# Attention followed by a rational feed-forward: x of two batches kept as one float32 plane, split into rounded part and remainder only in the feed-forward

## The chip, the core and the metric

The kernel runs on one core of a Trainium2 chip. The metric is the device time of one execution in microseconds (us), as the median of several runs.

## What is computed

Four batches of 448 tokens, 12 heads of 64, all float32. The scores of all heads are mixed by a 12x12 matrix before the softmax and again after it; the feed-forward has 768 -> 2048 -> 768 with a quotient of two polynomials as its activation.

```python
scores = scale * np.matmul(q, k.transpose(0, 1, 3, 2))
scores = np.einsum('bhij,hg->bgij', scores, w_pre)
attn = np.exp(scores - np.max(scores, axis=-1, keepdims=True))
attn = attn / (np.sum(attn, axis=-1, keepdims=True) + 1e-09)
attn = np.einsum('bhij,hg->bgij', attn, w_post)
x = np.matmul(attn, v)            # -> [1792, 768] after moving the heads
h = x @ w_in
P = a[0] + a[1]*h + a[2]*h**2 + a[3]*h**3
Q = 1.0 + abs(b[0])*abs(h) + abs(b[1])*h**2
out = (P / (Q + 1e-6)) @ w_out
```

## The kernel before

**Two parts.** Attention goes over 16 tiles T of query rows (`T // 4` is the batch b; a batch has three tiles of 120 rows and a short one, the first in batch 0, the last in the others). A tile has 6 groups of two blocks (a short one 5), 92 groups in all, each with one `put_pre` (mix before the softmax, L599), the softmax, and one `put_post` (mix after it, L674). `put_qk` (L498) makes the scores of a coming tile, `d<-st` DMAs of SP (L520) shuffle them into the tile `d`, and `put_av` (L739) multiplies with v, three times a tile, the first time two groups after the tile's own groups. The feed-forward then goes over 64 units u, u = 0 to 63: four chunks c of hidden columns, in each chunk four turns (one batch each, in the order of the list `orders`), in each turn four units of 128 hidden columns.

**x and its two planes.** The feed-forward multiplies in float32r, with an operand in two parts: a rounded plane hi and a remainder plane lo = x - hi. A unit's first product `m1` (18 matmuls, L918) uses both planes of x of one batch. In `put_av` ACT (ScalarE) rounds the result out of PSUM into hi (`hi`, L236) and DVE (VectorE) subtracts it to make lo (`lo`, L757). Both planes of a batch, 2688 KB, are stored by SP to `x_scr[b]`, in eight DMAs (L762). `xs` is one buffer, so a batch can write its x only when the stores of the batch before are done.

**Loads in the feed-forward.** `put_load_x` (L899) loads both planes of a turn's batch in one DMA of 2688 KB. There are two homes, the tile `xs` and the tile `d` of attention; `held` and `homes` say which load serves which turn. Turn 0 uses load 1 (into `d`), turn 1 the last batch of attention, still in `xs`, turn 2 load 2 (into `d`, free after turn 0's last m1), turn 3 load 3 (into `xs`, free after turn 1's last m1). So units 0 to 3 are turn 0, units 8 to 11 are turn 2, units 12 to 15 turn 3.

**A unit's chain.** m1 -> on ACT m, sq, ua (L931, L934, L937) and the denominator (L941) -> DVE -> Ln and Exp on ACT (L954, L958) -> DVE -> g, rounded (L236 or L238) and remainder (L978) -> six second products `m2` of three matmuls each (L1008) into the banks ps_t, ps_u, ps_a, which hold a turn's output. At a turn's end ACT or DVE copy the output to tiles `o`; in chunk 0 SP stores them to `o_scr`, in chunks 1 and 2 GpSimd (POOL) adds them there with an accumulating DMA (L1059), and the last chunk adds them on DVE.

**Order.** Nothing is scheduled at run time. Each operation is recorded with a duration, dependencies and a wished time `at`; `Plan.run` lists them per engine, lets operations that may run on ACT or DVE go where they start first, and the program is written in that order. Each engine, and SP's and POOL's queue of DMAs, then runs its list strictly in order.

```python
orders = [(0, 3, 1, 2), (2, 1, 0, 3), (3, 0, 1, 2), (2, 1, 0, 3)]
held = [1, 0, 2, 3, 3, 2, 4, 5, 5, 4, 6, 7, 7, 6, 8, 9]
```

Of the kernel before, what the change touches and what calls it, by code (L numbers as in the profile page):

```python
# [18 lines left out]
B, H, S, D = 4, 12, 448, 64  # L19
# [9 lines left out]
NT = 4 * B  # L29
# [3 lines left out]
KD = DM // 128  # L33
# [21 lines left out]
class Plan:  # L55
# [163 lines left out]
def dma(nbytes):  # L219
    return nbytes / 300e3  # L220
# [21 lines left out]
def mixed_attention_then_rational_ffn(ctx: ExitStack, tc, q, k, v, w, wmix, mask, a, b2, out):  # L242
# [481 lines left out]
    def put_av(T, pr, at):  # L724

        b, n, r, c0 = T // 4, rows[T], real[T], row0[T]
        if pr == 0:
            sums[T] = {}, [R["ps_" + holds[T]].take() for _ in range(2)]
        box, slots = sums[T]
# [14 lines left out]
        def part(hv):  # L744
            return box[hv][:, 0:3 * n].rearrange("p (r w) -> p r w", r=3)[:, :, 0:r]

        def hi(hv):
            def fn(eng):
                if hv == 0 and T % 4 == 0:
                    Xs[b] = sb["xs"].tile([128, 2, 2, 3, S], F32R, tag="xs", name="xs")  # L750
                move(nc, eng, Xs[b][:, hv, 0, :, c0:c0 + r], part(hv))
            return fn

        def lo(hv):
            def fn():
                x = Xs[b][:, hv, :, :, c0:c0 + r]
                nc.vector.tensor_sub(x[:, 1], part(hv), x[:, 0].bitcast(F32))  # L757
            return fn

        def store(hv, hl, cols):  # L760
# [9 lines left out]
            return  # L770
        for hv in range(2):
            deps, after = [o], []
            if hv == 0 and T % 4 == 0:
                deps.append(R["xs"].take())
            else:
                after.append(xs_op[b][0])
            h_ = add(copies(3 * n, False, on=ON["x_hi"]), 0, hi(hv), deps, at=at, after=after)
            l_ = add("dve", dve(3 * n), lo(hv), [h_], at=at)
            xs_op.setdefault(b, []).append(h_)
            x_done.setdefault((b, hv), []).append(l_)  # L780
            R["ps_" + holds[T]].uses[slots[hv].k].append(l_)
            if T % 4 > 1:
                last = T % 4 == 3
                cols, done = (slice(c0, S), x_done[b, hv][3:]) if last else (slice(0, c0 + r), x_done[b, hv][:])
                for hl in range(2):
                    when = at + (3.0 if last else 5.0) + (1.6 if last else 4.0) * (2 * hl + hv)
                    s_ = bulk(0.45, store(hv, hl, cols), done, at=when, nbytes=128 * 3 * max(cols.stop - cols.start, 240) * 4, late=1.0, since=when - 1.0)
                    x_st.setdefault(b, []).append(s_)
                    R["xs"].uses[b + 1].append(s_)

    xs_op, x_done = {}, {}
    x_st = {}

    LEAD = {1: 15.0, 2: 9.0, 3: 15.0}
    put_warm(8, -20.0)
# [66 lines left out]
    x_use = {0: R["xs"].uses[B]}  # L862
    x_ld[0] = x_done[B - 1, 0] + x_done[B - 1, 1]
    o_use, o_st = {}, {}
    m1_op = {}
# [25 lines left out]
    def put_load_x(n, at):  # L891
        b, name = homes[n]

        def fn():
# [265 lines left out]
```

## Time and profile before

| what | value |
|---|---|
| median of 3 runs (lowest to highest) | 826.3 us (825.48 to 827.0) |
| the profiled execution's own time | 822.94 us |
| its span, first to last instruction | 821.2 us |
| granted TensorE clock, mean of the span | 0.998 |
| busy: PE, DVE, ACT, POOL | 799.4, 692.3, 502.0, 223.7 us |
| moved by DMA | 155.46 MB |

The profiled execution is 1.7 us longer than its span, and 3.4 us under the median of the runs. Shares of busy time are means over two unlike parts: attention fills the first 340 us, the feed-forward the rest. A matmul's duration as listed overlaps that of its neighbours, so the distance between two starts tells more than the sum.

### The profile page before, as it was taken

Reading aid. Unit: us, or ns where it says so; the run is one execution under the profiler, and the core shown is the slowest. Engines: PE = TensorE matmul, PEld = TensorE weight load, DVE = VectorE, ACT = ScalarE, POOL = GpSimd, SP = SyncE. Lnnn points to the kernel's source line nnn. Section 1 sums busy time; section 2 is a strip of 40 time slices with the busy share of each in tenths; the row PEclk is TensorE's granted clock in tenths of the full one; section 3 lists DMA queues with packets and bytes.
Section 4 is the critical chain, followed back from the end, with each engine's and each line's share of the span. In section 5 each row is a group of like instructions: output and inputs, shape, how many; then the busy total and the mean of one; then the engine's idle time right before and its main releaser. Section 6 shows DMA issues by size and latency. Waiting matters only on the chain.

```text
span 821.2 us, 23269 instructions
## 1 busy us (share of the span) xinstructions
PE 799.4 (97%) x9368; PEld 598.1 (73%) x9368; DVE 692.3 (84%) x1252; ACT 502.0 (61%) x1099; POOL 223.7 (27%) x394
## 2 busy tenths in 40 slices
PE   7899999999999999999999999999999999999998
PEld 2245555554454454689999999999999999999997
DVE  6777788888887888788999998999989998777775
ACT  2557666656665666666777776677657676545632
POOL 2334444434343445611211212222212222100000
PEclk9999999999999999999999999999999999999999
DMA  6777887668877865974733275656467534466314
GB/s 219 254 215 235 259 280 236 209 199 281 266 212 210 269 192 189 352 243 192 257 126 100 75 255 126 188 124 125 84 215 212 152 81 67 94 221 224 128 52 157
DMA packets 72332, 155.46 MB, mean 189 GB/s; under 512 B 12608, under 2 KB 53152, under 8 KB 71072
## 3 DMA queue, kind: packets, MB, share of 16 engines
q1 hardware_dynamic: 68468, 142.47, 52.6%
q0 software_dynamic: 3456, 11.01, 8.2%
q8 instruction: 74, 1.21, 0.6%
q10 hardware_dynamic: 300, 0.48, 0.2%
q14 instruction: 34, 0.28, 0.1%
HBM read 77.49 MB, written 37.75 MB: 140 GB/s over the span
## 4 chain that ended last, share of the span: by engine, by line
PE 87%; DVE 5%; DMA 3%; ACT 2%; issue 1%; POOL 1%; SPq 0%; ACTq 0%; POOLq 0%; DVEq 0%
PE ps_s L918 29%; PE ps_u L1008 10%; PE ps_t L1008 9%; PE ps_a L1008 9%; PE ps_s L498 8%; PE ps_a L674 8%; PE ps_u L599 4%; PE ps_t L599 4%; PE ps_u L739 3%; PE ps_t L739 2%; ACT e L614 2%; DVE nm L605 2%; DMA d<-st 1%; DVE aa L690 1%; DMA kk<-in_k 1%
## 5 line engine op out<-in xcount | busy, mean ns | idle before, releaser
L690 DVE STREAM_TRANSPOSE aa<-ps_a 128x448 f32<-128x448 f32 (+1 forms) x184 | 107.7, 618 | 11.7 <-PE ps_a L674 11.2
L918 PE MATMUL ps_s<-d,w 128*128 128x448 f32 x504 | 107.3, 366 | 0.0
L918 PE MATMUL ps_s<-xs,w 128*128 128x448 f32 x504 | 107.1, 366 | 0.0
L447 POOL TENSOR_TENSOR w<-cm,w 128x384 fp32r<-128x384 f32 x48 | 56.0, 1167 | 171.9 <-ACT w L236 165.0
L918 PEld LDWEIGHTS ps_s<-d,w 128*128 128x128 f32 x504 | 94.3, 188 | 8.8 <-issue 0.7
L918 PEld LDWEIGHTS ps_s<-xs,w 128*128 128x128 f32 x504 | 94.6, 188 | 7.9
L634 POOL TENSOR_SCALAR krs<-kpost,rr 128x64 f32<-128x64 f32 x180 | 80.8, 462 | 69.2 <-DVE rr L625 48.0
L674 PEld LDWEIGHTS ps_a<-e,krs 64*32 64x32 f32 x2880 | 44.9, 106 | 74.7 <-issue 26.6
L674 PE MATMUL ps_a<-e,krs 64*32 64x224 f32 x2880 | 93.2, 355 | 1.5 <-DVE aa L690 0.8
L236 ACT COPY st<-ps_s 120x448 f32<-120x448 f32 (+1 forms) x115 | 57.6, 533 | 57.8 <-PE ps_s L498 30.5
L931 ACT ACTIVATE m<-ps_s,a_sb 128x448 f32<-128x448 f32 x64 | 46.3, 723 | 76.1 <-PE ps_s L918 72.7
L498 PE MATMUL ps_s<-kk,q 64*64 64x448 f32 x696 | 90.2, 548 | 0.3 <-DVE st L238 0.3
L1008 PE MATMUL ps_u<-g,w 128*128 128x448 f32 x336 | 84.1, 366 | 0.0
L1008 PE MATMUL ps_a<-g,w 128*128 128x448 f32 x336 | 84.1, 366 | 0.0
L1008 PE MATMUL ps_t<-g,w 128*128 128x448 f32 x336 | 83.9, 366 | 0.0
L614 ACT ACTIVATE e<-ps_t,nm 128x448 f32<-128x448 f32 x92 | 57.7, 634 | 31.1 <-DVE nm L605 28.0
L614 ACT ACTIVATE e<-ps_u,nm 128x448 f32<-128x448 f32 x88 | 55.2, 633 | 28.9 <-DVE nm L605 24.6
L1008 PEld LDWEIGHTS ps_t<-g,w 128*128 128x128 f32 x336 | 63.1, 188 | 5.3
L1008 PEld LDWEIGHTS ps_a<-g,w 128*128 128x128 f32 x336 | 63.1, 188 | 5.2
L1008 PEld LDWEIGHTS ps_u<-g,w 128*128 128x128 f32 x336 | 63.1, 188 | 5.2
L961 DVE TENSOR_TENSOR sq<-sq,ua 128x448 f32<-128x448 f32 x64 | 41.4, 648 | 19.4 <-ACT ua L958 19.1
L954 ACT ACTIVATE ua<-sq 128x448 f32<-128x448 f32 x64 | 37.1, 580 | 33.9 <-DVE sq L951 33.6
(94 smaller groups left out, 1445.1 us busy)
## 6 DMA issues: line engine op xcount, KB each, us to landing
d<-st SPq DMA_DIRECT2D x144, 210.0 KB
cr<-in_w SPq DMA_DIRECT2D x64, 384.0 KB
d<-x_scr SPq DMA_DIRECT2D x5, 2688.0 KB
xs<-x_scr SPq DMA_DIRECT2D x4, 2688.0 KB
o_scr<-o POOLq DMA_DIRECT2D x24, 448.0 KB, 5.5
d<-st SPq DMA_DIRECT2D x45, 157.5 KB
x_scr<-xs SPq DMA_DIRECT2D x12, 540.0 KB
q<-in_q SPq DMA_DIRECT2D x16, 384.0 KB
```

The costliest lines, as they stand in the source:

```text
L236: eng.copy(o, i)
L447: eng.tensor_sub(t[:, 1, :], box["m"].bitcast(F32), t[:, 0, :].bitcast(F32))
L498: nc.tensor.matmul(box["s"][hh][i0:i1, 0:S], lhsT=Q[T][d, pr, i0:i1], rhs=K[b][d, pr, :], start=True, stop=True)
L599: nc.tensor.matmul(box[r if nt == 2 else 0]["t"][64 * c:64 * c + 64, 0:S], lhsT=kpre[p], rhs=Dt[T][p, kb + c if nt == 2 else kb, :], start ...
L614: nc.scalar.activation(e, box[r]["t"][:, 0:S], AF.Exp, bias=box[0]["nm"][:, r:r + 1], accum_out=box[0]["sm"][:, r:r + 1])
L634: eng.tensor_scalar_mul(box[r]["kr"], kpost, rr)
L674: nc.tensor.matmul(banks[c]["p"][q_:q_ + BT, JH * r:JH * (r + 1)], lhsT=box[r]["kr"][p, m_, :], rhs=box[r]["e"][p, JH * jh:JH * (jh + 1)], ...
L690: nc.vector.transpose(o, src)
L918: nc.tensor.matmul(h[:, 0:S], lhsT=W[fi][:, wi, kk * 128:(kk + 1) * 128], rhs=x[:, kk // 3, xj, kk % 3, :], start=(n == 0), stop=(n == 3 * ...
L931: nc.scalar.activation(new("m"), box["h"], AF.Identity, scale=a_sb[:, 3:4], bias=a_sb[:, 2:3])
L961: nc.vector.tensor_mul(box["vv"], box["vv"], box["rc"])
L1008: nc.tensor.matmul(O[key][:, 0:S], lhsT=W[fi][:, wi, DM + m * 128:DM + (m + 1) * 128], rhs=box["g"][:, gi, :], start=(f == 0 and n == 0), ...
```

## The change

For batches 0 and 1 (`PLAIN`) attention copies x out of PSUM as plain float32; the copies of both batches lie in the one tile `xs` (each takes half of it), DVE's subtraction falls away, and six DMAs store one plane of 1344 KB to `y_scr[b]` when the batch is finished. The order of the turns is permuted so that batches 2 and 3 are the first two and batches 0 and 1 come third and fourth; every `held` entry stays. When batch 0 or 1 is loaded for the first time, `put_load_x` does, for each half hv of the features: SP loads y into the hi plane (672 KB); ACT writes its rounded negative into the lo plane (`minus`, three pieces) and rounds the hi plane in place (`hi`, three pieces); a DMA issued by GpSimd adds y onto the lo plane (`rest_of`, 672 KB, `accum_op=add`), which leaves the remainder; SP stores both planes of the half (1344 KB) to `x_scr[b]`, from where later turns load as before. m1 of the turn waits for all roundings and both adding DMAs.

```diff
+PLAIN = (0, 1)
...
+    y_scr = {b: dram.tile([128, 2, 3, S], F32, name=f"y_scr{b}") for b in PLAIN}
...
-                move(nc, eng, Xs[b][:, hv, 0, :, c0:c0 + r], part(hv))
+                    if b != PLAIN[1]:
+                        Xs[b] = sb["xs"].tile([128, 2, 2, 3, S], F32R, tag="xs", name="xs")
+                    if plain:
+                        i = PLAIN.index(b)
+                        Y[b] = Xs[PLAIN[0]].rearrange("p v l k s -> p (v l) k s").bitcast(F32)[:, 2 * i:2 * i + 2]
+                move(nc, eng, Y[b][:, hv, :, c0:c0 + r] if plain else Xs[b][:, hv, 0, :, c0:c0 + r], part(hv))
...
-            l_ = add("dve", dve(3 * n), lo(hv), [h_], at=at)
+            l_ = h_ if plain else add("dve", dve(3 * n), lo(hv), [h_], at=at)
...
+            if plain:
+                for kk in range(3 if T % 4 == 3 else 0):
+                    when = at + 3.0 + 1.6 * (3 * hv + kk)
+                    s_ = bulk(0.45, store_y(hv, kk), x_done[b, hv][:], at=when, nbytes=128 * S * 4, late=1.0, since=when - 1.0)
...
-    orders = [(0, 3, 1, 2), (2, 1, 0, 3), (3, 0, 1, 2), (2, 1, 0, 3)]
+    orders = [(2, 3, 0, 1), (1, 0, 2, 3), (3, 2, 0, 1), (1, 0, 2, 3)]
...
+        def load(hv):
+                nc.sync.dma_start(out=X[n][:, hv, 0].bitcast(F32), in_=y_scr[b][:, hv])
+        def minus(hv, kk):
+                nc.scalar.activation(X[n][:, hv, 1, kk], X[n][:, hv, 0, kk].bitcast(F32), AF.Copy, scale=-1.0)
+        def hi(hv, kk):
+                nc.scalar.copy(X[n][:, hv, 0, kk], X[n][:, hv, 0, kk].bitcast(F32))
+        def rest_of(hv):
+                nc.gpsimd.dma_start(out=X[n][:, hv, 1].bitcast(F32), in_=y_scr[b][:, hv], accum_op=ALU.add)
+        def store(hv):
+                nc.sync.dma_start(out=x_scr[b][:, hv], in_=X[n][:, hv].bitcast(F32))
...
+            got.append(bulk(0.5, load(hv), [*free, y_st[b]], at=at + hv, nbytes=128 * 3 * S * 4, after=got[:1]))
...
+                neg.append(add("act", act(S), minus(hv, kk), [got[hv]], at=when))
+                his.append(add("act", act(S), hi(hv, kk), neg[-1:], at=when))
+            o = add("pool", 1.1, rest_of(hv), neg, at=at + 5.0 + 1.6 * 3 * hv, extra=5.0)
+            x_ld[n] += [*his, o]
+            s_ = bulk(0.63, store(hv), [*his, o], at=at + 15.0 + 1.6 * 3 * (hv + 1), nbytes=128 * 2 * 3 * S * 4)
```

The program's order moves with it at three places. The first is PE's list from the m1 of unit 7 to the m1 of unit 8, the first of turn 2 (`ps_s` is an m1, the other banks are m2 products). Before:

```order
L918 MATMUL ps_s<-xs,d 128x448 x18
L1008 MATMUL ps_u<-g,d 128x448 x3
L1008 MATMUL ps_t<-g,w_6172 128x448 x3
L1008 MATMUL ps_a<-g,d 128x448 x3
L1008 MATMUL ps_t<-g,w_6172 128x448 x3
L1008 MATMUL ps_a<-g,d 128x448 x3
L1008 MATMUL ps_u<-g,w_6172 128x448 x6
L918 MATMUL ps_s<-d,w_6172 128x448 x18
```

And with the change, to the m1 of unit 9:

```order
L985 MATMUL ps_s<-xs,d 128x448 x18
L1075 MATMUL ps_u<-g,w_6153 128x448 x3
L1075 MATMUL ps_a<-g,w_6153 128x448 x6
L1075 MATMUL ps_t<-g,w_6277 128x448 x6
L1075 MATMUL ps_u<-g,w_6277 128x448 x6
L1075 MATMUL ps_a<-g,w_6277 128x448 x3
L985 MATMUL ps_s<-d,w_6153 128x448 x18
L1075 MATMUL ps_a<-g,w_6277 128x448 x3
L985 MATMUL ps_s<-d,w_6277 128x448 x18
```

There were 6 products m2 between the m1 of units 6 and 7 and 7 between those of units 7 and 8; now there are 12 and 8, so the m1 of unit 8 stands seven products later, and the m1 of unit 9 one product behind it instead of twelve.

The second place is ACT's list in the same stretch, from the first copy of turn 0's output (`o<-ps_t`) to behind the Exp of unit 5 (L958, now L1025). Before:

```order
L236 COPY o<-ps_t 128x448
L236 CAST g<-ua 128x448
L411 ACTIVATE cm<-cr 128x384
L236 COPY o<-ps_u 128x448
L411 ACTIVATE cm<-cr 128x384
L931 ACTIVATE m<-ps_s,a_sb 128x448
L954 ACTIVATE ua<-sq 128x448
L934 ACTIVATE sq<-ps_s 128x448
L958 ACTIVATE ua<-ua 128x448
```

With the change (L940 is `minus`, L945 is `hi`):

```order
L237 COPY o<-ps_t 128x448
L237 CAST g<-ua 128x448
L940 ACTIVATE d<-d 128x448 x2
L237 COPY o<-ps_u 128x448
L945 CAST d<-d 128x448
L237 CAST w_6989<-cm 128x384
L237 COPY o<-ps_a 128x448
L413 ACTIVATE cm<-cr 128x384
L1021 ACTIVATE ua<-sq 128x448
L945 CAST d<-d 128x448
L1025 ACTIVATE ua<-ua 128x448
L940 ACTIVATE d<-d 128x448 x2
```

The first `L940 x2` here is the last `minus` of half 0 and the first of half 1; the second, behind unit 5's Exp, is the last two of half 1, for which the second adding DMA waits. The copies of x push in among the units' own steps, and m of unit 6 moves behind them.

The third is SP's list from turn 2's load on. Before:

```order
L899 DMA d<-x_scr_123 128x5376
L406 DMA cr<-in_w 128x768 x3
L1054 DMA o_scr_126<-o 128x896
L406 DMA cr<-in_w 128x768
L899 DMA xs<-x_scr_124 128x5376
L1054 DMA o_scr_126<-o 128x896 x2
```

With the change:

```order
L935 DMA d<-y_scr_126 128x1344
L408 DMA cr<-in_w 128x768
L935 DMA d<-y_scr_126 128x1344
L408 DMA cr<-in_w 128x768 x2
L1121 DMA o_scr_130<-o 128x896 x2
L408 DMA cr<-in_w 128x768
L1121 DMA o_scr_130<-o 128x896
L955 DMA x_scr_122<-d 128x2688
L935 DMA xs<-y_scr_127 128x1344
L408 DMA cr<-in_w 128x768
L955 DMA x_scr_122<-d 128x2688
L935 DMA xs<-y_scr_127 128x1344
```

One load has become two with a weight load between them, and each store of a finished half (L955), which waits for that half's adding DMA, stands ahead of one half's load for turn 3.

## Rows read from the trace of the kernel before

**Rows 1.** The page: shares of the chain that ended last.

```profile
PE 87%; DVE 5%; DMA 3%; ACT 2%; issue 1%; POOL 1%; SPq 0%; ACTq 0%; POOLq 0%; DVEq 0%
```

**Rows 2.** Windows: stretch, length, busy us (x instructions), PEclk, DMA share, GB/s.

```profile
core 0: us, PE busy (x) PEld busy (x) DVE busy (x) ACT busy (x) POOL busy (x), PEclk, DMA share, GB/s
62.00:125.00 63.00, 62.30 (x1392) 31.46 (x1376) 51.18 (x96) 43.25 (x117) 27.54 (x61) 1.00 0.81 258
125.00:209.00 84.00, 82.13 (x1776) 42.02 (x1768) 70.49 (x131) 50.43 (x136) 35.56 (x76) 1.00 0.75 231
339.70:817.00 477.30, 477.30 (x2612) 438.38 (x2612) 415.68 (x749) 299.92 (x562) 83.16 (x82) 1.00 0.52 156
```

**Rows 3.** Timeline of PE: first products with v of T = 0, 4, 8, 12.

```profile
42.58 1.35 PE L739 MATMUL ps_u<-aa,vv 64*64 64x90 f32 x56
...
125.02 1.70 PE L739 MATMUL ps_u<-aa,vv 64*64 64x120 f32 x56
...
208.95 1.69 PE L739 MATMUL ps_t<-aa,vv 64*64 64x120 f32 x56
...
292.42 1.79 PE L739 MATMUL ps_u<-aa,vv 64*64 64x120 f32 x54
```

**Rows 4.** Timeline of PE, 157 to 208 us: start, us, instruction, [idle before].

```profile
157.00 0.93 PE L498 MATMUL ps_s<-kk,q 64*64 64x448 f32 x8
...
158.78 1.24 PE L498 MATMUL ps_s<-kk,q 64*64 64x448 f32 x8
...
160.74 1.21 PE L498 MATMUL ps_s<-kk,q 64*64 64x448 f32 x8
...
182.82 0.98 PE L599 MATMUL ps_u<-d,kpre 64*64 64x448 f32 x8 [0.51 <-DVE xs L757]
...
200.23 0.98 PE L599 MATMUL ps_u<-d,kpre 64*64 64x448 f32 x8 [0.57 <-DMA x_scr<-xs]
...
204.48 1.42 PE L674 MATMUL ps_a<-e,krs 64*32 64x224 f32 x32
...
207.59 1.42 PE L674 MATMUL ps_a<-e,krs 64*32 64x224 f32 x32
```

**Rows 5.** Groups by line: busy us, mean ns, idle before and its releaser.

```profile
L757 DVE TENSOR_TENSOR xs<-ps_u,xs 128x360 fp32r<-128x360 f32 (+1 forms) x18 | 8.2, 490 | 4.4 <-ACT xs L236 4.0 <-DMA d<-st 0.4
L757 DVE TENSOR_TENSOR xs<-ps_t,xs 128x360 fp32r<-128x360 f32 (+1 forms) x14 | 6.8, 513 | 4.5 <-ACT xs L236 4.4
L236 ACT CAST xs<-ps_u 128x360 fp32r<-128x360 f32 (+1 forms) x18 | 6.9, 436 | 3.4 <-PE ps_u L739 3.2
L236 ACT CAST g<-ua 128x448 fp32r<-128x448 f32 x36 | 20.5, 568 | 30.7 <-DVE ua L968 26.0 <-PE ps_a L1008 4.1
```

**Rows 6.** DMA queues and issues: count, KB each, median us to landing.

```profile
q0 software_dynamic: 3456, 11.01, 8.2%
d<-x_scr SPq DMA_DIRECT2D x5, 2688.0 KB
o_scr<-o POOLq DMA_DIRECT2D x24, 448.0 KB, 5.5
x_scr<-xs SPq DMA_DIRECT2D x12, 540.0 KB
```

**Rows 7.** Timeline of PE: m1 of units 3, 6, 8, 12, and one m2.

```profile
359.72 3.92 PE L918 MATMUL ps_s<-d 128*128 128x448 f32 x18
...
380.04 3.84 PE L918 MATMUL ps_s<-xs,w 128*128 128x448 f32 x18
...
386.15 0.78 PE L1008 MATMUL ps_a<-g,w 128*128 128x448 f32 x3
...
395.29 3.84 PE L918 MATMUL ps_s<-d,w 128*128 128x448 f32 x18
...
428.34 3.84 PE L918 MATMUL ps_s<-xs,w 128*128 128x448 f32 x18
```

**Rows 8.** Timeline of ACT: first output copy of turn 0; Exp of units 5 and 9.

```profile
385.13 0.53 ACT L236 COPY o<-ps_t 128x448 f32<-128x448 f32 x1 [1.14 <-PE ps_t L1008]
385.56 0.58 ACT L236 CAST g<-ua 128x448 fp32r<-128x448 f32 x1
...
389.95 0.59 ACT L958 ACTIVATE ua<-ua 128x448 f32<-128x448 f32 x1
...
416.87 0.57 ACT L958 ACTIVATE ua<-ua 128x448 f32<-128x448 f32 x1
```

**Rows 9.** Timeline of SP: load of turn 2; the weight load behind it.

```profile
365.63 1.49 SPq L899 DMA_DIRECT2D d<-x_scr  x1
369.43 12.27 SPq L406 DMA_DIRECT2D cr<-in_w  x3
```

**Rows 10.** Tile o_scr: POOL's adding DMAs of 448 KB, and their landing.

```profile
L1059 POOL DMA_DIRECT2D o_scr<-o x24: 858/872/1063, 500.3 to 716.1; - x24
...
DMA to landing us min/median/max: 5.0/5.5/11.2
```

**Rows 11.** One of them beside a load of x: SP, POOL, then its landing.

```profile
597.27 0.33 SPq L899 DMA_DIRECT2D d<-x_scr  x1
...
599.57 0.88 POOL L1059 DMA_DIRECT2D o_scr<-o  x1 [1.68 <-ACT o L236]
...
o_scr<-o POOLq DMA_DIRECT2D x1, 448.0 KB, 11.2
```

More of the change, by code (lines that the diff above doesn't have):

```diff
@@ L726, in put_av @@
         b, n, r, c0 = T // 4, rows[T], real[T], row0[T]
+        plain = b in PLAIN
         if pr == 0:
@@ L749, in fn @@
                 if hv == 0 and T % 4 == 0:
-                    Xs[b] = sb["xs"].tile([128, 2, 2, 3, S], F32R, tag="xs", name="xs")
-                move(nc, eng, Xs[b][:, hv, 0, :, c0:c0 + r], part(hv))
+                    if b != PLAIN[1]:
[4 more added lines that the diff above has]
+                move(nc, eng, Y[b][:, hv, :, c0:c0 + r] if plain else Xs[b][:, hv, 0, :, c0:c0 + r], part(hv))
             return fn
@@ L757, in fn, with store_y @@
                 nc.vector.tensor_sub(x[:, 1], part(hv), x[:, 0].bitcast(F32))
+            return fn
+        def store_y(hv, kk):
+            def fn():
+                nc.sync.dma_start(out=y_scr[b][:, hv, kk], in_=Y[b][:, hv, kk])
             return fn
@@ L772, in put_av @@
             deps, after = [o], []
-            if hv == 0 and T % 4 == 0:
+            if hv == 0 and T % 4 == 0 and b == PLAIN[1]:
+                after.append(xs_op[PLAIN[0]][0])
+            elif hv == 0 and T % 4 == 0:
                 deps.append(R["xs"].take())
@@ L781, in put_av @@
             R["ps_" + holds[T]].uses[slots[hv].k].append(l_)
-            if T % 4 > 1:
+            if plain:
+                for kk in range(3 if T % 4 == 3 else 0):
+                    when = at + 3.0 + 1.6 * (3 * hv + kk)
+                    s_ = bulk(0.45, store_y(hv, kk), x_done[b, hv][:], at=when, nbytes=128 * S * 4, late=1.0, since=when - 1.0)
+                    y_st.setdefault(b, []).append(s_)
+                    R["xs"].uses[-1].append(s_)
+            elif T % 4 > 1:
                 last = T % 4 == 3
@@ L788, in put_av @@
                     x_st.setdefault(b, []).append(s_)
-                    R["xs"].uses[b + 1].append(s_)
+                    R["xs"].uses[-1].append(s_)
     xs_op, x_done = {}, {}
-    x_st = {}
+    x_st, y_st, Y = {}, {}, {}
     LEAD = {1: 15.0, 2: 9.0, 3: 15.0}
@@ L861, in mixed_attention_then_rational_ffn @@
     x_ld, m2_op, o_ev = {}, {}, {}
-    x_use = {0: R["xs"].uses[B]}
+    x_use = {0: R["xs"].uses[-1]}
     x_ld[0] = x_done[B - 1, 0] + x_done[B - 1, 1]
@@ L892, in put_load_x, with home @@
         b, name = homes[n]
-        def fn():
+        def home():
             if name == "x":
@@ L898, in fn @@
                 t = sb[name].tile([128, 2, 2, 3, S], F32R, tag=name, name=name)
-            nc.sync.dma_start(out=t.bitcast(F32), in_=x_scr[b])
             X[n] = t
-        x_ld[n] = [add(
-            "sp", 0.63, fn, [R[name].take(), R["d"].uses[NT - 2] if n == 1 else op_rest, x_st[b]], at=at, extra=dma(128 * 2 * KD * S * 4))]
+        def fn():
+            home()
+            nc.sync.dma_start(out=X[n].bitcast(F32), in_=x_scr[b])
+        free = [R[name].take(), R["d"].uses[NT - 2] if n == 1 else op_rest]
         x_use[n] = R[name].uses[-1]
+        if b in x_st:
+            x_ld[n] = [add("sp", 0.63, fn, [*free, x_st[b]], at=at, extra=dma(128 * 2 * KD * S * 4))]
+            return
+        def load(hv):
+            def fn():
+                if hv == 0:
+                    home()
+                nc.sync.dma_start(out=X[n][:, hv, 0].bitcast(F32), in_=y_scr[b][:, hv])
+            return fn
+        def minus(hv, kk):
+            def fn():
+                nc.scalar.activation(X[n][:, hv, 1, kk], X[n][:, hv, 0, kk].bitcast(F32), AF.Copy, scale=-1.0)
+            return fn
+        def hi(hv, kk):
+            def fn():
+                nc.scalar.copy(X[n][:, hv, 0, kk], X[n][:, hv, 0, kk].bitcast(F32))
+            return fn
+        def rest_of(hv):
+            def fn():
+                nc.gpsimd.dma_start(out=X[n][:, hv, 1].bitcast(F32), in_=y_scr[b][:, hv], accum_op=ALU.add)
+            return fn
+        def store(hv):
+            def fn():
+                nc.sync.dma_start(out=x_scr[b][:, hv], in_=X[n][:, hv].bitcast(F32))
+            return fn
+        x_ld[n], x_st[b], got = [], [], []
+        for hv in range(2):
+            got.append(bulk(0.5, load(hv), [*free, y_st[b]], at=at + hv, nbytes=128 * 3 * S * 4, after=got[:1]))
+            his, neg = [], []
+            for kk in range(3):
+                when = at + 5.0 + 1.6 * (3 * hv + kk)
+                neg.append(add("act", act(S), minus(hv, kk), [got[hv]], at=when))
[3 more added lines that the diff above has]
+            s_ = bulk(0.63, store(hv), [*his, o], at=at + 15.0 + 1.6 * 3 * (hv + 1), nbytes=128 * 2 * 3 * S * 4)
+            x_st[b].append(s_)
+            x_use[n].append(s_)
     def put_unit(u):
```

## The prediction

> **What bounds the kernel now.** I read the chain that ended last first: 87% of it lies on PE [rows 1], so an edit counts for what it does to PE's list. The windows then part the program [rows 2]. In the feed-forward (339.7 to 817 us) PE is busy for 477.30 of 477.30 us at a granted clock of 1.00: nothing is to be gained there, and whatever makes an m1 late is lost in full. In attention the window 62 to 125 us is nearly as dense (62.30 of 63.00), while 125 to 209 us has 82.13 of 84.00. The first products with v of T = 0, 4, 8 and 12 [rows 3] measure it better, since a busy PE may be a slow one. From T = 0 to 4 lie 24 groups in 82.44 us, 3.435 a group. From 4 to 8 lie 23 groups, so 79.0 us, and it takes 83.9: 4.9 us too long. From 8 to 12 it takes 83.5, 4.5 too long. The timeline of PE [rows 4] shows some of the excess of the second stretch: an idle 0.51 us that a subtraction of x (L757) ended, an idle 0.57 that a store of x ended, score products of 1.24 and 1.21 us where the like takes 0.93, and two products L674 of 1.42 us.
>
> **Attention, part by part.** Of 32 subtractions, 8.2 + 6.8 = 15.0 us of DVE [rows 5], 16 go: 7.5 us of DVE, most of it beside a busy PE. What of it lies on the path: the two idle times, 0.51 + 0.57 = 1.08; the stretch of the two score products, 0.31 + 0.28 = 0.59; for the two slow L674 I put 0.4, an estimate from the stretch of the score products. That is 2.1 us. Bounds: the idle time that names the subtraction alone, 0.5, below, and the whole excess, 4.9, above. A loss I exclude, as nothing is added to PE, DVE or ACT there. I take their middle, **2.7**: a little more than the 2.1 that I can point to, since delays of a tenth can't be listed. The copies on ACT stay as many; they waited 3.2 of 3.4 us for PE and hardly for a buffer [rows 5], so the new sharing of `xs` is worth nothing by itself. The stores shrink from 540 KB by 12 (the row has those of one shape) [rows 6] to planes of half the bytes; this is SP's and the DMA engines' work and is counted in the 0.57. The permuted order costs nothing as far as the first two turns go: the last batch of attention is still the second turn, and the first is again a batch that was stored long before.
>
> **Feed-forward, what is added.** 24 operations on ACT (`minus` and `hi`, twelve a batch) at 0.57, the price of a cast of the same 128x448 [rows 5], are 13.7 us of an engine that is busy 299.92 of 477.30 [rows 2]. Some output copies move to DVE, busy 415.68. Both stay under PE, so in sum they are free; their place is what can cost. The loads are covered: turn 2's was issued at 365.63, with weight loads behind it [rows 9]. Now a half-load of y and, behind a weight load, the other half stand there; three weight loads in a row took 12.27 us, so one between may hold the second half until some 371, and ACT wants it after 385.
>
> *When m1 of unit 8 can start.* From the m1 of unit 6 (380.04) to that of unit 8 (395.29) lie 75 matmuls in 15.25 us [rows 7]: 0.203 each, 0.61 for an m2, 3.66 for an m1 (their listed 0.78 and 3.84 overlap the next). The m1 of unit 8 now stands seven m2 later: 395.29 + 4.27 = **399.6**, with no loss, for the same products are only in another order.
>
> *When its x is ready.* After the copy from ps_t and a cast at 385.13 and 385.56 [rows 8], ACT has the last `minus` of half 0 and the first of half 1, then must wait to copy ps_a, which by PE's list is complete nine m2 after the m1 of unit 6: 380.04 + 45 x 0.203 = 389.2. Then come that copy, a weight's remainder, Ln, a `hi`, unit 5's Exp and two `minus`, seven instructions. ACT's starts lay 0.43 apart where it ran without a wait [rows 8], its casts last 0.44 to 0.57 [rows 5]; at 0.47 each they end at 392.5. (Unit 5's Exp starts at 391.1 instead of 389.95; its products stand behind the m1 of unit 7, at 380.04 + 72 x 0.203 = 394.7, and still have their g.) POOL issues the second adding DMA at 392.6, as its own issues take 0.87 us within the landing [rows 10].
>
> *How long that DMA takes* no row shows; adding DMAs of 448 KB land after 5.0 to 11.2 us, median 5.5 [rows 10]. Their queue was busy 8.2% of the span, 0.082 x 821.2 / 24 = 2.8 us for each [rows 6], so half as many bytes again add 1.4: 6.9 undisturbed. The lower bound is 5.0 (ready at 397.6), the upper 11.2 + 1.4 = 12.6 (405.2, a stall of 5.6). The 11.2 was beside a load of 2688 KB that SP had issued 2.3 us earlier [rows 11], 5.7 over the median. Here the neighbour is the store of half 0, 1344 KB, which SP may issue when the first adding DMA lands (issued about 386.6, landed 393.5): about 0.9 us behind the second, with half the bytes. Half the bytes would be +2.9; as it comes later I take a third of that, +0.9. So 7.8 us, ready at 400.4, and m1 of unit 8 **0.8 late**. Behind this wait PE has the m1 of unit 9 and all later products, so the 0.8 is lost whole.
>
> *Turn 3.* From the m1 of unit 8 to that of unit 12 it took 33.05 us [rows 7]; now four m1 and 23 m2 lie between, 141 x 0.203 = 28.7, so 428.3 plus the stall. The last `minus` of its x stands right behind unit 9's Exp, before at 416.87 [rows 8]; as late again as unit 5's, that is 418.0 + 0.57 + 0.94 = 419.5, and with 0.1 and 7.8 it is ready at 427.4: nothing, with 0.9 to spare. On SP the half-loads for turn 3 wait behind the stores of the finished halves, until 393.5 and 400.4; the tile `xs` is only free at 394.7 anyway, and its first `minus` is after 410. Nothing, while that cover of 10 us holds. The first m1 of turn 2 used `d`, free since unit 3's m1 at 359.72 [rows 7]: nothing.
>
> The Trainium skill ("DMA: Bandwidth & Descriptors", Anatomy of one DMA) fits such a transfer as 2.0 us plus its bytes over 436e3. By that 448 KB would take an estimated 3.05 us, where no landing in [rows 10] is under 5.0, so the trace decides; by the page 672 KB would land in 3.6, no m1 would wait, and the sum would be the 2.7 alone, 823.6, still within my forecast's case.
>
> **Sum.** -2.7 + 0.8 = -1.9. The profiled execution took 822.94 us, the median of the runs is 826.3, 3.4 above it. Taken off both, 821.0 for such an execution and **824.4** for the median. Later turns load x as before.
>
> **Rivals.** *The adding DMA is hidden and attention gives its whole excess back.* -4.9 and no stall: 821.4. For it: both idle times at PE name x, a landing of 6.9 would be in time, and the excess begins with the first batch that finds an earlier one's stores in `xs` [rows 3], which batch 1 now no longer does. Against: from T = 0 to 4 the same subtractions stand beside a dense PE [rows 2, 3], so they can't explain 4.9 by themselves, and ACT's copies into `xs` hardly waited for a buffer [rows 5].
>
> *Attention gives nothing.* This evidence pushed to its end: the subtractions lie beside the path, and another wait takes the place of the two named. Then +0.8 is left: 827.1, no change; 826.3 with the DMA in time, 827.8 with a stall of 1.5.
>
> *The store delays the adding DMA, slower.* Place: the m1 of units 8 and 12. If the store of half 0 costs the second adding DMA what half of the load did in [rows 11], +2.9, it lands after 9.8: ready at 402.4, a stall of 2.8 at unit 8. At unit 12 the Exp of unit 9 moves with the stall, so the same landing costs 419.6 + 9.8 - 428.3 = 1.1 more. Net -2.7 + 3.9 = +1.2, 827.5; with attention's 0.5 instead, 829.7, slower; with a landing of 11.2 (4.2 and 2.5) and attention's 2.7, 830.3. With attention's 2.7 it decides from landings of some 10 us on (3.0 + 1.3 of stalls); with 10.5 and 2.1 of attention the sum is +3.2, **829.5**, which I take for the case. For it: [rows 11] is the one landing beside x, and it doubled. Against: the median is 5.5, over 24 landings that also met loads of weights.
> The Trainium skill (same page, SWDGE vs HWDGE vs iDMA) says that each DMA engine serves its queues in turn, so a store from SP and an adding DMA from POOL share each engine. The trace agrees as far as 11.2 against 5.5 in [rows 10] goes.
>
> That the change doesn't do what it says is the smallest case: the list shows the subtractions gone and `minus` there.
>
> **How the numbers follow.** A measurement of this kernel can tell 0.2%, 1.65 us, from no change: under 824.65 is faster, over 827.95 slower. My forecast's case (attention 2.1 to 3.5, stall 0 to 1.5) has 0.45 and its own range 822.8 to 825.7; about two thirds of it, 0.3, is faster, 0.15 the same. The first rival 0.17, faster. Attention without gain 0.18, the same. The store as a brake 0.19, of it 0.18 slower. That it does something else 0.01. In sum: faster 0.47, same 0.34, slower 0.19. Leaving out a tenth on each side, the range goes from 821.9, inside the first rival, to 829.4, inside the last.
>
> **What would show it.** In the changed profile the distance from T = 4 to 8 should fall from 83.9 to about 81.2, the two idle times of [rows 4] should be gone, and from 0 to 4 nothing should change. PE should show an idle time before the m1 of unit 8 ended by POOL's adding DMA, 0 to 1.5 us, and none before that of unit 12. The landing of y's adding DMAs should be near 7 to 8 us, the second of a pair longer than the first. Wrong would be: 125 to 209 as long as before (the second rival), landings of 10 us and over (the third), or PE waiting before m2 products of units 5 to 8 for a g that ACT's new work made late.

## The result: slower by half a per cent

Over 20 runs each the median went from 829.5 to 833.6 us; the ratio is 1.0054, with a 95% interval from 1.0029 to 1.0080. I had forecast 824.4 and a range up to 829.4. Of the 9.2 us between 824.4 and 833.6, 3.2 are the base: the three runs of before that the forecast started from had a median of 826.3. The profile shown of before is of an execution quicker than all 20 runs (822.94 us, their lowest 825.03) and that of e2 below of a slow one (839.49), so the result is read part by part, and the feed-forward of e2 is not compared with the others.

The page and the windows of the changed kernel, which answer to [rows 1, 2]:

```profile
PE 84%; DMA 7%; DVE 4%; ACT 3%; issue 1%; SPq 0%; POOL 0%; ACTq 0%; DVEq 0%; POOLq 0%
```

```profile
core 0: us, PE busy (x) PEld busy (x) DVE busy (x) ACT busy (x) POOL busy (x), PEclk, DMA share, GB/s
62.00:125.00 63.00, 62.06 (x1372) 31.23 (x1368) 49.97 (x92) 41.37 (x112) 27.56 (x61) 1.00 0.72 221
125.00:209.00 84.00, 81.34 (x1793) 41.58 (x1796) 66.97 (x122) 51.82 (x139) 35.26 (x77) 1.00 0.73 225
346.20:828.00 481.80, 477.50 (x2611) 437.44 (x2610) 417.85 (x751) 310.08 (x582) 86.02 (x86) 1.00 0.56 165
```

In the feed-forward, which had not one gap before, PE is now idle for 4.30 of 481.80 us. The timeline of PE around units 8 to 10 shows 4.28 of it:

```profile
406.37 2.20 PE L985 MATMUL ps_s<-d,w 128*128 128x448 f32 x10
411.64 1.90 PE L985 MATMUL ps_s<-d,w 128*128 128x448 f32 x8 [3.07 <-DMA d<-y_scr]
...
413.99 3.84 PE L985 MATMUL ps_s<-d,w 128*128 128x448 f32 x18
...
420.88 3.93 PE L985 MATMUL ps_s<-d,w 128*128 128x448 f32 x18 [1.21 <-DVE m L1014]
```

The first ten matmuls of the m1 of unit 8 run (nine use half 0 of x, the tenth the rounded plane of half 1). The other eight wait 3.07 us for the remainder plane of half 1, which the second adding DMA writes. The m1 of unit 9 follows with one m2 between, and that of unit 10 then waits 1.21 us until DVE has read the PSUM bank that it writes. POOL, SP and the landing of the second adding DMA (the us from its issue to its end):

```profile
393.42 1.06 POOL L950 DMA_DIRECT2D d<-y_scr  x1 [3.92 <-ACT d L940]
...
399.84 0.88 POOL L950 DMA_DIRECT2D d<-y_scr  x1 [3.27 <-ACT d L940]
```

```profile
398.51 0.32 SPq L1121 DMA_DIRECT2D o_scr<-o  x1
401.00 0.32 SPq L955 DMA_DIRECT2D x_scr<-d  x1
401.64 0.32 SPq L935 DMA_DIRECT2D xs<-y_scr  x1
402.06 1.52 SPq L408 DMA_DIRECT2D cr<-in_w  x1
```

```profile
d<-y_scr POOLq DMA_DIRECT2D x1, 672.0 KB, 11.8
```

It landed after 11.8 us. Four transfers of SP lay beside it: an output store, the store of half 0 that I had counted, issued 1.2 us behind it, and then a half-load of y for turn 3 and a load of weights. For its first 1.2 us the first adding DMA was still running too. The other three adding DMAs landed after 7.6, 8.5 and 6.5 us.

Attention's part can't be read from one profile. By this one it lost 6.5 us: the first m1 of the feed-forward starts at 346.15, before at 339.69. The measure used below is therefore the **length of the feed-forward**, from the first m1's start to the end of the span: 821.2 - 339.69 = 481.5 us before, 832.6 - 346.15 = 486.5 now.

### The profile page after: what moved, and what is told of

Same layout as the page of the kernel before. It is cut to its first block, busy times and chain, and to the rows that moved or that the text cites. A ratio compares the mean times of both kernels' runs of the same rounds, so it can differ in the third digit from the quotient of the medians.

```text
span 832.6 us, 23262 instructions
## 1 busy us (share of the span) xinstructions
PE 801.2 (96%) x9368; PEld 597.5 (72%) x9368; DVE 690.3 (83%) x1241; ACT 511.4 (61%) x1118; POOL 226.5 (27%) x398
## 3 DMA queue, kind: packets, MB, share of 16 engines
q8 instruction: 74, 1.21, 0.6%
## 4 chain that ended last, share of the span: by engine, by line
PE 84%; DMA 7%; DVE 4%; ACT 3%; issue 1%; SPq 0%; POOL 0%; ACTq 0%; DVEq 0%; POOLq 0%
PE ps_s L985 27%; PE ps_u L1075 9%; PE ps_t L1075 9%; PE ps_a L1075 9%; PE ps_s L500 8%; PE ps_a L676 8%; PE ps_t L601 4%; PE ps_u L601 4%; PE ps_u L742 3%; DMA d<-st 3%; ACT e L616 2%; PE ps_t L742 2%; DVE nm L607 1%; DMA xs<-y_scr 1%; DMA cr<-in_w 1%
## 5 line engine op out<-in xcount | busy, mean ns | idle before, releaser
L607 DVE TENSOR_REDUCE nm<-ps_t 128x2 f32<-128x896 f32 (+1 forms) x47 | 49.7, 1057 | 13.6 <-PE ps_t L601 12.2
L607 DVE TENSOR_REDUCE nm<-ps_u 128x2 f32<-128x896 f32 (+1 forms) x45 | 47.5, 1056 | 14.3 <-PE ps_u L601 12.5
```

The source lines that it names most:

```text
L607: nc.vector.tensor_reduce(out=nm[:, 0:nt], in_=box[0]["both"][:, 0:nt, 0:S], axis=AX.X, op=ALU.max, negate=True)
```

## The experiments

| kernel | ratio to before (95%) | first m1 starts | feed-forward, us |
|---|---|---|---|
| before | | 339.69 | 481.5 |
| changed | 1.0054 (1.0029 to 1.0080) | 346.15 | 486.5 |
| e1_no_split | 1.0024 (0.9995 to 1.0054) | 346.99 | 482.8 |
| e2_store_late | 1.0020 (0.9989 to 1.0051) | 351.28 | 486.4 |
| e3_minus_early | 0.9997 (0.9966 to 1.0028) | 350.43 | 483.2 |
| e4_pool_subtracts | 1.0047 (1.0012 to 1.0082) | 340.80 | 487.7 |
| e5_quiet | 0.9995 (0.9959 to 1.0030) | 347.88 | 482.7 |
| e6_tuned | 1.0021 (0.9986 to 1.0057) | 339.42 | 485.4 |
| e7_before_again | 0.9990 (0.9961 to 1.0018) | 346.88 | 481.5 |
| e8_quiet_early | 1.0027 (0.9993 to 1.0060) | 348.63 | 481.9 |
| e9_changed_again | 1.0047 (1.0016 to 1.0078) | 346.65 | 488.3 |
| e10_store_only | one run | 348.60 | 487.9 |
| e11_loads_only | one run | 346.80 | 483.3 |

Two theories stood against each other: A, the feed-forward waits for the split; B, attention itself became slower. All kernels but e7, which is before again, have the changed attention, on PE instruction for instruction.

**No split.** y is loaded into both planes of x, without `minus`, `hi`, the adding DMAs and the stores; the remainder plane then holds y itself.

```diff
-    minus(hv, kk), hi(hv, kk), rest_of(hv), store(hv)
+    nc.sync.dma_start(out=X[n][:, hv, 1].bitcast(F32), in_=y_scr[b][:, hv])
```

> Leaves out: the split of x of batches 0 and 1; y is loaded into both planes each time, so the remainder plane holds y itself (no minus, no rounding, no adding DMA, no store). Attention is that of the changed kernel, instruction for instruction. Theory A (the loss is the wait of the m1 of units 8 and 10 in the feed-forward, 3.1 + 1.2 us): no idle time of PE from 400 us on, the stretch T = 8 to 12 back near 84 us since its 89 was chance, and the time within 0.2% of before or up to 2 us faster. Theory B (attention itself became slower, by the 5 to 6 us that the profile shows between T = 8 and 12): that stretch stays near 89, and the time is 2 to 6 us above before although PE waits for nothing in the feed-forward.

PE's list there has one idle time left in the feed-forward:

```profile
410.04 3.94 PE L982 MATMUL ps_s<-d,w 128*128 128x448 f32 x18 [0.61 <-DVE m L1011]
```

So 3.7 of the 5.0 us belong to the split, with what it does to PE's order: without it the plan puts the m1 of unit 8 at 56.7 us of the feed-forward instead of 60.2. The wait that is left is that of unit 9, whose m1 stands three m2 behind that of unit 8. The time, 1.0024, lies just above A's 0.2% and at the lower end of B's. The stretch from T = 8 to 12 stayed long, 89.3 us, as B said; but in the kernels that follow, with the same attention, it came out as 83.1 to 88.6, and in before's second run as 86.8. One profile can't tell A from B there.

**The store of half 0 later.** Both stores wait for both adding DMAs of the turn.

```diff
-            s_ = bulk(0.63, store(hv), [*his, o], at=at + 15.0 + 1.6 * 3 * (hv + 1), ...)
+        for hv in range(2):
+            s_ = bulk(0.63, store(hv), x_ld[n][:], at=at + 25.0 + 1.6 * 3 * (hv + 1), ...)
```

> The store of half 0 to x_scr waits for both adding DMAs of a turn, so that it no longer moves beside the second one; nothing else is edited. Theory A1 (the store of 1344 KB beside it made the second adding DMA land after 11.8 us): landing 7 to 8 us, the wait of the m1 of unit 8 is 0 to 0.5 us, and the time 3 to 4 us under the changed kernel. Theory A2 (the second adding DMA is just issued too late by ACT's list, and other transfers beside it, the load of y for turn 3 and a weight load, slow it as much): landing still 10 us or more, PE waits 2 us or more, time within 1.5 us of the changed kernel. Theory B: no change either way, 833 to 834.

The edit didn't do what I wrote of it. The plan orders by both adding DMAs, but in the program the store of half 0 waits only for its own half's, and as SP came to it, it started: 3.6 us behind the second adding DMA (issued at 404.95), with both half-loads of turn 3 ahead of it. SP, and what PE then waited:

```profile
406.81 1.10 SPq L935 DMA_DIRECT2D xs<-y_scr  x2
408.02 0.44 SPq L408 DMA_DIRECT2D cr<-in_w  x1
408.56 0.91 SPq L955 DMA_DIRECT2D x_scr<-d  x1
```

```profile
415.80 2.58 PE L986 MATMUL ps_s<-d,w 128*128 128x448 f32 x8 [2.06 <-DMA d<-y_scr]
```

```profile
412.00:420.00 8.00, 5.94 (x22) 5.07 (x21) 6.50 (x12) 5.05 (x12) 1.01 (x1) 0.80 1.02 391
```

The landing was 10.8 us and the wait 1 us shorter, but the mean granted clock was 0.80 in the window with the wait and what follows it (those eight matmuls took 2.58 us, in the changed kernel 1.90). This run doesn't tell store and loads apart; two runs at the end go further.

**`minus` earlier.**

```diff
-                when = at + 5.0 + 1.6 * (3 * hv + kk)
+                when = at + 0.1 * (3 * hv + kk)
```

> The wished times of minus and of the rounding are moved 5 to 13 us earlier, so ACT does them as soon as y has landed, and the adding DMAs are issued earlier; the store of half 0 still follows the first of them. Theories A1 and A2: the second adding DMA is issued some 5 us before its place in the changed kernel, lands in time even if it takes 10 us, PE waits 0 to 0.5 us at unit 8 and unit 10; time 3 to 4.5 us under the changed kernel, unless ACT's earlier work makes a g late (then a wait of PE before an m2 of units 4 to 7 shows it). Theory B: 833 to 834.

SP's store of half 0, and the landing of the second adding DMA:

```profile
400.67 0.33 SPq L955 DMA_DIRECT2D x_scr<-d  x1
```

```profile
d<-y_scr POOLq DMA_DIRECT2D x1, 672.0 KB, 9.8
```

The second adding DMA was issued 47.9 us behind the first m1 (398.37 - 350.43), 5.8 us sooner than in the changed kernel (399.84 - 346.15 = 53.7). It took 9.8 us, 2.0 less than in the changed kernel, although the store of half 0 lay beside it here too, issued 2.3 us behind it instead of 1.2. No m1 waited for it; three waits of 0.2 to 0.4 us for DVE and ACT are left. The time is that of before.

**GpSimd subtracts.** y goes into the lo plane, ACT rounds it into hi, and POOL subtracts in place: no adding DMA and no `minus`.

```diff
-                nc.gpsimd.dma_start(out=X[n][:, hv, 1].bitcast(F32), in_=y_scr[b][:, hv], accum_op=ALU.add)
+                nc.gpsimd.tensor_sub(x[:, 1], x[:, 1].bitcast(F32), x[:, 0].bitcast(F32))
```

> No adding DMA: y is loaded into the lo plane, ACT rounds it into the hi plane, and GpSimd subtracts hi from it in place, twelve subtractions of 128x448 in all at some 1.3 us, beside the remainders of the weights that it makes anyway. Theory A: x is ready some 8 us sooner, no wait of PE at units 8 to 12, time 4 to 5 us under the changed kernel and so within 0.2% of before, or 1 to 2 us faster if attention gained. Theory B: 833 to 834.

A miss. No m1 waits for x, but other waits sum to 4.35 us (the feed-forward is 6.2 longer than before). The first two of them:

```profile
390.73 0.47 PE L1075 MATMUL ps_t<-g,w 128*128 128x448 f32 x1 [1.22 <-ACT g L237]
391.66 0.69 PE L1075 MATMUL ps_t<-g,w 128*128 128x448 f32 x2 [0.47 <-DVE g L1045]
```

The chains of g and m became late. One thing that slows them is seen in the timelines of DVE and POOL: the same DVE operation takes 0.67 us alone and 1.57 when it starts beside one of the new subtractions (L951).

```profile
380.70 1.57 DVE L1035 SCALAR_TENSOR_TENSOR ua<-m,a_sb,ua 128x448 f32<-128x448 f32 x1
...
389.40 0.67 DVE L1035 SCALAR_TENSOR_TENSOR ua<-m,a_sb,ua 128x448 f32<-128x448 f32 x1
```

```profile
380.52 1.27 POOL L951 TENSOR_TENSOR d<-d 128x448 fp32r<-128x448 f32 x1
```

The Trainium skill ("Advanced Engine Details and Errata", GPSIMD Details) says that the Pool engine shares a read and a write interface with DVE and conflicts with its instructions that have two inputs in SBUF; this pair agrees. It is not new in kind: beside POOL's remainder of a weight the like operation took 1.48 us in before, too. How much of the 4.35 us comes from the added subtractions, and how much from the changed order of ACT, was not tried.

**Nothing large beside it.** SP issues the store of half 1 first, which waits for the second adding DMA, and the half-loads of turn 3 behind both stores.

```diff
+        for hv in (1, 0):
+            s_ = bulk(0.63, store(hv), x_ld[n][:], at=at + 10.0 - hv, ..., after=quiet[1:])
+            quiet.append(s_)
...
-            got.append(bulk(..., after=got[:1]))
+            got.append(bulk(..., after=[*got[:1], *quiet[:2]]))
```

> Both stores of a turn's halves to x_scr and both half-loads of y for turn 3 stand on SP behind a store that waits for the second adding DMA, so nothing large moves beside it; the adding DMAs themselves are issued where they were. Theory A1/A2 joined (any large transfer beside it stretches the second adding DMA): it lands after 6.5 to 8 us instead of 11.8 and 10.8, so x is ready for the second half of the m1 of unit 8, which stood at 408.2 less the attention's shift, and PE waits 0 to 0.3 us there. Rival A3 (an adding DMA of 672 KB takes 10 to 12 us by itself): landing still 10 us or more, PE waits 2 us or more. Time by A1/A2 2 to 4 us under the changed kernel, by A3 the same as it.

```profile
400.24 0.32 SPq L1125 DMA_DIRECT2D o_scr<-o  x1
402.10 0.33 SPq L408 DMA_DIRECT2D cr<-in_w  x1
411.18 0.80 SPq L957 DMA_DIRECT2D x_scr<-d  x2
```

```profile
411.17 1.90 PE L989 MATMUL ps_s<-d,w 128*128 128x448 f32 x8 [0.86 <-DMA d<-y_scr]
```

It was issued at 401.57 and x was there at 411.17, so it took 9.6 us, between the two expectations. An output store and a load of weights are still beside it, and so is the end of the first adding DMA, which, issued at 395.14, landed after 7.6 us. The wait fell from 3.07 to 0.86, the feed-forward from 486.5 to 482.7, and unit 10 no longer waits.

**A smaller move of the split, with 9 us planned for the DMA.**

```diff
+                when = at + 4.0 + 0.8 * (3 * hv + kk)
...
+                his.append(add("act", act(S), hi(hv, kk), neg[-1:], at=when + 4.0))
+            o = add("pool", 1.1, rest_of(hv), neg, at=at + 4.0 + 0.8 * 3 * hv, extra=9.0)
```

> minus is wished 1 us earlier and in steps of 0.8 us, the rounding 4 us behind it, and the plan takes 9 us instead of 5 for the adding DMA; all else is the changed kernel. If the loss of the feed-forward is only the late adding DMA, PE waits for no adding DMA, and less than in the run with all of the split moved early for DVE or ACT (there 0.8 us in three waits): feed-forward from the first m1 to the end 482 to 483 us (before 481.5, changed 486.5), the time 828 to 830. If ACT's additional work makes g late whatever its place, waits of PE of 1 us or more before m2 products or an m1 between units 4 and 12.

A miss: no wait for an adding DMA. The second one landed in time after 9.7 us, with the first long done and the store of half 0 issued 4.5 us behind it. But there are idle times of 0.76 for m, 0.76 and 0.53 for g, and the feed-forward is 485.4. These waits make 2.05 of the 3.9 us over before; the rest was not traced. Where ACT's added operations stand can cost nearly as much as the DMA. Its profiled execution took 826.6 us, by an attention that ended at 339.42; its median was 831.2.

**Before, again.**

> The kernel before, unedited, for the spread: time equal to before within 0.2%; its feed-forward from the first m1 to the end again 481 to 482 us without an idle time of PE; the start of the first m1 anywhere from 338 to 351 us, as the kernels with the changed attention, equal to each other instruction for instruction there, showed 340.8 to 351.3. If its attention is by far steadier than theirs, 339 to 342, the changed attention is the one that costs, and theory B is back.

```profile
183.41 0.98 PE L599 MATMUL ps_u<-d,kpre 64*64 64x448 f32 x8 [0.52 <-DVE xs L757]
...
204.11 0.98 PE L599 MATMUL ps_u<-d,kpre 64*64 64x448 f32 x8 [2.56 <-DMA kk<-in_k]
...
228.08 0.98 PE L599 MATMUL ps_t<-d,kpre 64*64 64x448 f32 x8 [2.47 <-DMA kk<-in_k]
...
346.88 3.95 PE L918 MATMUL ps_s<-d,w 128*128 128x448 f32 x18
```

The feed-forward is the same to 0.1 us; attention is 7.2 us longer than in the profile that I read, 5.0 of it by two waits for loads of k that weren't there. So before spreads in the same way as its variants, and B has nothing left but the one profile it was drawn from. The idle time that the subtraction ended came back (0.52, [rows 4] 0.51), the one that a store of x ended did not. The two slow score products of [rows 4] came back too, to the hundredth, and at their place in the changed kernel stand shorter ones. Before's second run, then the changed kernel:

```profile
159.82 1.24 PE L498 MATMUL ps_s<-kk,q 64*64 64x448 f32 x8
...
161.78 1.21 PE L498 MATMUL ps_s<-kk,q 64*64 64x448 f32 x8
```

```profile
159.66 1.12 PE L500 MATMUL ps_s<-kk,q 64*64 64x448 f32 x8
...
161.56 0.98 PE L500 MATMUL ps_s<-kk,q 64*64 64x448 f32 x8
```

**Both repairs.**

```diff
+                when = at + 4.0 + 1.2 * (3 * hv + kk)
...
+                his.append(add("act", act(S), hi(hv, kk), neg[-1:], at=when + 6.0))
+            o = add("pool", 1.1, rest_of(hv), neg, at=at + 4.0 + 1.2 * 3 * hv, extra=8.0)
```

> The run with nothing large beside the second adding DMA, and with it the three last minus of a pair wished some 3 us earlier, each rounding 6 us behind its minus, and 8 us planned for the adding DMA. The sum of the two repairs: the second adding DMA is issued 2 to 4 us before its place in the changed kernel and lands in 8 to 10 us; PE waits for it 0 us; feed-forward from the first m1 to the end 481.8 to 483.0 us (before 481.5, changed 486.5, quiet alone 482.7). Time, with attention at the mean of the seven runs that share it: 828.5 to 830.5. If ACT's moved work makes a g or an m late instead, as in the run with the planned 9 us, the feed-forward stays at 484 or more.

```profile
408.81 3.84 PE L989 MATMUL ps_s<-d,w 128*128 128x448 f32 x18
```

The m1 of unit 8 runs in one piece; the second adding DMA, issued at 398.96, landed after 8.3 us. The feed-forward is 481.9 us, 0.4 above before, with no idle time of PE of 0.2 us or more. The time, 831.9, missed the expectation of 828.5 to 830.5 and can't be told from before.

**The changed kernel, again.**

> The changed kernel, unedited, to see whether its wait comes back: if the second adding DMA is late by construction (theory A), PE waits 2 to 4 us in the second half of the m1 of unit 8 and the feed-forward takes 485 to 487.5 us, and the time is 833 to 834.5 at the median. If 11.8 us was chance, the landing is 7 to 9 us and the feed-forward 482 to 484. Attention: its first m1 anywhere from 339 to 351.

```profile
412.14 3.35 PE L985 MATMUL ps_s<-d,w 128*128 128x448 f32 x8 [3.09 <-DMA d<-y_scr]
```

```profile
411.00:414.00 3.00, 1.86 (x5) 1.69 (x6) 2.28 (x6) 0.18 (x1) 0.00 (x0) 0.54 1.04 425
414.00:417.00 3.00, 3.00 (x10) 2.65 (x9) 0.00 (x0) 3.00 (x7) 0.00 (x0) 0.50 1.00 338
```

The landing was 11.8 us again and the wait 3.09 us: it is in the order of the program. This time the granted clock was at half, the lower of its two levels (1.2 GHz), behind the wait, and the same eight matmuls took 3.35 us instead of 1.90. Unit 10 did not wait here, and still the feed-forward was 1.8 us longer than in the first profile.

**Store or loads.** In the first of two kernels only the half-loads of turn 3 are moved behind the store of half 1; in the second only the two stores, that of half 1 issued first.

```diff
+        before = quiet[:]
...
-            got.append(bulk(..., after=got[:1]))
+            got.append(bulk(..., after=[*got[:1], *before]))
...
+            quiet.append(s_)
```

```diff
+        for hv in (1, 0):
+            s_ = bulk(0.63, store(hv), x_ld[n][:], at=at + 30.0 - hv, ..., after=[s_] if s_ else [])
```

> Only the half-loads of y for turn 3 are moved behind the store of half 1, which waits for the second adding DMA; the store of half 0 (1344 KB) stays beside it, as in the changed kernel, with a load of weights. If what counts is all the bytes beside it: 1728 KB beside it here, 2400 KB in the changed kernel (11.8 us) and 384 KB in the quiet one (9.6), so a landing of 10.5 to 11.2 us and a wait of PE of 1.8 to 2.5 us. If the store is what counts (A1): 11.5 us or more and a wait near 3. If the loads are (A2'): 9.6 to 10 and a wait under 1.2.

> Only the stores are moved, and this time truly: SP issues that of half 1 first, which waits for the second adding DMA itself (in the run with the late store, half 0's still started 3.6 us behind it). Both half-loads of y for turn 3 (1344 KB) and a load of weights lie beside it. If all the bytes count: the same 1728 KB, 10.3 to 11.2 us and a wait of 1.5 to 2.5. If the store is what counts (A1): 9.6 to 10 us and a wait under 1.2. If the loads are: 10.8 or more.

POOL's second adding DMA, SP's store behind it, and PE in the first:

```profile
402.28 0.88 POOL L952 DMA_DIRECT2D d<-y_scr  x1 [3.27 <-ACT d L942]
```

```profile
403.50 0.32 SPq L957 DMA_DIRECT2D x_scr<-d  x1
```

```profile
414.25 3.35 PE L989 MATMUL ps_s<-d,w 128*128 128x448 f32 x8 [3.17 <-DMA d<-y_scr]
```

The same in the second, with the two half-loads:

```profile
400.48 0.88 POOL L950 DMA_DIRECT2D d<-y_scr  x1 [3.27 <-ACT d L940]
```

```profile
402.35 1.59 SPq L935 DMA_DIRECT2D xs<-y_scr  x2
```

```profile
410.55 1.90 PE L987 MATMUL ps_s<-d,w 128*128 128x448 f32 x8 [1.28 <-DMA d<-y_scr]
```

The landings were 11.9 and 10.0 us. Equal numbers of bytes lay beside it, so the number of bytes alone doesn't decide: the store by itself gives the whole wait of the changed kernel, the loads 0.4 us over the quiet kernel's landing. A1, that the store is what counts, stands for the changed kernel, and with the store there the loads of turn 3 are free. That a store is dearer than loads isn't shown by this: the store began 1.2 us behind the adding DMA, the loads 1.9 us, and in the run with `minus` earlier a store that began 2.3 us behind left the landing at 9.8.

**What they say together.** In the order of the changed kernel the second adding DMA lands after 9.6 us with nothing large beside it, 10.0 with the loads and 11.8 to 11.9 with the store of half 0 from 1.2 us on. Issued earlier it landed after 8.3 (e8), 9.7 (e6) and 9.8 us (e3), the last two with the store beginning later beside it. So the price of a neighbour hangs on more than what it is; when it starts is the nearest guess, and was not varied by itself. The four kernels in which x is in time or nearly so and no other wait is over 0.7 us (e1, e3, e5, e8) average a ratio of 1.0011, the two runs of the changed kernel 1.0050. The difference, 0.4% or some 3 us, known to about 2, is what repairing the split's wait gave in the runs; in the profiles the same four have 482.6 us of feed-forward, 3.8 and 5.6 under the changed kernel's two. Of the 0.9 us by which the four stand over before, their feed-forward explains 1.1. For attention -0.2 us is left, known to about 1.5 us either way: no gain that these runs can show, nor a loss. No version was measurably faster than the kernel before.

## Why the prediction was wrong

Two terms of the sum failed: the landing of the second adding DMA, 7.8 us forecast and 11.8 measured, and attention's gain, 2.7 forecast and none that the runs show. The rival "the store delays the adding DMA", which had 0.19, is the one that came true, with a larger landing than it was priced at (9.8 to 11.2), and beside it the rival "attention gives nothing".

- **Where the m1 of unit 8 stands**: right. Forecast 399.6; it started at 406.37, and with the 6.46 us (346.15 - 339.69) taken off by which the feed-forward began later, at 399.9.
- **When the second adding DMA is issued**: 392.6 forecast, 399.84 - 6.46 = 393.4. Off by 0.8.
- **How long it takes**: this is the step that failed first. 7.8 forecast, 11.8 measured, twice. The undisturbed 6.9 was fair for an adding DMA alone (6.1 to 6.6 at best in seven of the nine profiles with one, 7.3 in the other two). For the second of a pair at this place it was not: with the end of the first, an output store and weights beside it, it took 9.6. Which of them makes the 2.7 us was not tried (in turn 3, second ones whose twin still ran landed after 7.3 to 9.8). And the price of the store was read from [rows 11] as +2.9 for half the bytes and then cut to a third because it starts later; from the place that I had foreseen (0.9 us behind, measured 1.2) it is 11.9 - 9.6 = +2.3. The cut was a guess, though a store that begins still later (e3) does seem to cost less.
- **What waits for it**: I let the whole m1 wait. Its first ten matmuls don't need the second adding DMA, so that was due some 2.2 us later than I had it, which hid part of the error. To the 0.8 forecast come 0.8 for the issue and 4.0 for the landing, less 2.2 and less the 0.3 by which the m1 stood later: 3.1 against 3.07.
- **What comes behind the wait**: 1.21 us at unit 10 were not foreseen. In this order two m1 stand one m2 apart, and DVE had not read a bank in time when the first was 3.07 us late; when it was 0.86 late (e5), unit 10 did not wait. Nor was the clock foreseen, which made the feed-forward 1.8 us longer in the second of the changed kernel's two profiles.
- **Turn 3**: right. No wait at unit 12.
- **Attention**: -2.7 forecast, none found in the runs. Part of what I pointed to is real: the 0.51 that a subtraction ended stands in both profiles of before and in none with the changed attention; the two score products take 1.24 and 1.21 in both of before and 1.12 and 0.98 in all eleven others; of the two slow L674 one is left in those. That is about 1 us by these rows, an estimate, and less than the runs can tell. The 0.57 of the store was one execution's. The stretch from T = 4 to 8, which I expected to fall from 83.9 to 81.2, was 83.2 in the first profile (126.17 to 209.32), 83.2 to 87.4 over the eleven profiles with the changed attention, and 86.5 in before's second run (126.34 to 212.82). Waits that come and go are larger than the term: 2.56 and 2.47 for loads of k in before's second run, and in the changed kernel's first profile 1.30 for ACT close to where the 0.51 had been. What makes the rest of the excess was not traced. The second rival, attention gives nothing, came nearest on this part.

## What to carry to other kernels

Before a term is read from a wait, ask whether the wait would be there in another execution: a part of the program without idle time repeated to 0.1 us here, a part that waits for DMAs spread over 11 us (first m1 from 339.42 to 350.43), and a gain of 2 us can't be read from one profile of the latter. A second profile of before, taken first, would have shown which of the rows repeat. A transfer on a path with little slack is priced with all that runs beside it, and not by bytes alone: here a store from 1.2 us on made it 2.3 us longer, and loads of as many bytes from 1.9 us on 0.4. Work that is moved out of a place with slack into a stage that runs without a gap has to bring its own slack: in the profiles' feed-forward the same split cost 5 us where it stood and 0.4 us when `minus` came 3 us sooner and SP kept the large transfers back.

## What the runs showed that I had not expected

An adding DMA keeps the DMA engines busy at a low rate. Windows of the changed kernel, the first with packets of the first adding DMA alone, the others with the second and its neighbours (the last three columns are clock, DMA share, GB/s):

```profile
396.00:399.00 3.00, 2.98 (x15) 2.44 (x14) 2.97 (x6) 2.80 (x7) 0.57 (x1) 1.00 0.89 154
...
402.00:405.00 3.00, 3.00 (x17) 2.66 (x16) 2.97 (x6) 3.00 (x7) 0.44 (x1) 1.00 1.09 353
405.00:408.00 3.00, 3.00 (x16) 2.75 (x15) 2.90 (x8) 3.00 (x7) 0.36 (x1) 1.00 1.02 317
```

At 0.89 of the engines' time it moves 154 GB/s, where a mixed stretch has 353 at 1.09. By that share it nearly fills the engines by itself, so there is little room beside it.

And of three idle times of PE at the same place, 3.07, 3.09 and 3.17 us, the first was followed by the full granted clock (2.4 GHz) and the other two by half of it. The first in the changed kernel, the third in e10:

```profile
411.60:414.60 3.00, 2.96 (x14) 2.74 (x15) 1.20 (x3) 1.30 (x3) 0.00 (x0) 1.00 1.05 428
```

```profile
414.20:417.20 3.00, 2.96 (x8) 2.65 (x9) 2.28 (x5) 0.32 (x1) 0.00 (x0) 0.50 0.80 316
```
